# Five loads issued ahead of the sixth pair's q and k on SyncE's queue

## The chip, the cores and the metric

The kernel runs on one core of a Trainium2 chip. The metric is the device time of one execution in microseconds (us). The kernel before has a median of 680.91 us over 3 runs (680.24 to 683.12).

## The reference, cut to what matters

Two kinds of attention are added, and their sum goes through two mixers:

```
q, k, v: (4, 8, 576, 64)                 # batch, heads, positions, width of a head
q_d, k_d, v_d = means of 4 neighbouring rows of q, k, v       # 144 rows
out   = repeat(softmax(q_d k_d^T / 8) v_d, 4)                 # pooled attention
out  += softmax(q k^T / 8, only where |i - j| < 4) v          # local attention
x     = out as (4, 576, 512)
u     = x + (relu(x^T w_tok1) w_tok2)^T                       # token mixer
x     = u + relu(u w_ch1) w_ch2                               # channel mixer
theta = x w_theta;  y = w_tok_r (x cos theta) + w_tok_i (x sin theta)
result = (x + y) + relu((x + y) w_ch)
```

The weights arrive as 64-bit floats and are turned on the chip into pairs of a high and a low part, so that a product takes three matmuls.

## The kernel before, in words

The 32 heads are worked as 16 pairs of heads (4 for each batch) and as 8 quads (two pairs each). In the attention each step is a generator: every `next` issues the instructions up to its next `yield`. A string, ORDER (lines 33 to 84), holds the names of the steps in the order in which they are advanced, and so the order in which the instructions stand on each engine's queue; nothing rearranges them in this stage (it is recorded under `tc.manual_schedule`). The last stage (from line 1356 on) is arranged by a scheduler.

The steps that the change names, each with what its first advance issues on SyncE (SP):

- `P5` (`load_pair`, line 375): q and k of pair 5, 582 KB, into one of 4 buffers `qk` in rotation; the buffer is free when TensorE and VectorE have done with pair 1, whose q and k it held.
- `W0` (`load_values`, line 382): the values of pair 0 as four DMAs, two of 32 partitions (146.2 KB each) and two of 6 partitions (27.4 KB each).
- `G1`, `G0` (`tok1`, line 333): 512 KB each of w_tok1; `G6` (`tok2`, line 347): 288 KB of w_tok2. All go through `converted` (line 166), whose line 187 issues the DMA; the conversion is in later advances.
- `V1` (`pool_values`, line 391): the values of quad 1 to be pooled, 650 KB, into the single buffer `vd`; it is free when GpSimd (POOL) has done the second addition of quad 0 (line 401).

The later advances of these steps use the data: `K5` (`pool_pair`, lines 421 and 422) adds neighbouring columns of pair 5's q and k on VectorE (DVE); `V1`'s next advance adds on POOL (line 398); `G1`, `G0` and `G6` convert on ScalarE (ACT) at lines 199 and 201 and on DVE at lines 203 to 215. `F0` (`quad_front`, lines 425 to 520) is the pooled attention of quad 0: its products end in `od` on TensorE (PE, lines 493 to 500), DVE divides them (lines 504 to 507) into `ods`, SP stores `ods` to memory (lines 510, 511) and loads it back, repeated, as `xu` (lines 516, 519). `L0` to `L3` (`pair_local`) is the local attention, with its scores at line 533.

Each DMA of SP bumps one of eight semaphores in turn (DMAHW0 to DMAHW7 in the rows of the order below), and waits until the DMA that used this semaphore before it, eight DMAs earlier, has landed.

Of the kernel before, what the change touches and what calls it, by code (L numbers as in the profile page):

```python
# [30 lines left out]
FIRST = 1  # L31
ROWS = ((8, 9), (0, 2), (4, 6), (2, 3))
ORDER = """
G3 P0 G2 I*2 P1 G3 P4 G3 V0 P2 G3 K0 G3 G2 I G2 I L0*2 P3 K1 F0 W1 L0 F0 L1 L0 G3 F0 V0 L1*2 P5 V0 L2 W0 G2 K2 V0 G2
F0 G1 L1 V1 F0 L2 K3 G0 G6 K4 L0 F0 L0 L2 L1 G2 F1 L2 K5 L1 L0 F0 F1 G1*2 F1 V1 F0*2 W3 L0 F1 G5 G0 L1 G0 F1 G6 F2 L1
G0 P6 W2 G5 G6 L3 V1 F2 V1 L3 G6 F2 F1 L3 G1 G4 F1 L2 P7 L5 L2 L5 F1 G1 L3 A0 V2 X0 A1 T0 L3 G1 L5 G0 L3 T0 G0 L2 G2
F1 G4 F2 G5 T0 K6 T0 V2 X2 L2 G6 W5 F2 K7 V2 L4*2 E0.0*2 T0 L4 V3 V2 A2 L3 E0.1 L5 G4 L4 W4 L5 G6 L5 G4 L3 X2 F3 G5 P8
P9 A3 G4 F2 G5 E0.1 T1 G4 G5 T0 F2 V3 L4 F3 F2 T0 L4 V3 X2 F3 L6 V3 L6 X7 T0 P11 L6 X2 X0 F3 K8 U0.0 L6 T0 X2 X0 U0.0
# [1419 lines left out]
```

## Time and profile before

| what | value |
|---|---|
| median of 3 runs | 680.91 us (680.24 to 683.12) |
| the profiled execution's own time | 686.51 us |
| its span, from the first instruction to the last | 684.7 us |
| PE busy | 657.2 us (96%), 7320 matmuls |
| DVE, ACT, POOL busy | 521.0, 321.1, 98.0 us |
| DMA moved | 109.93 MB, mean 161 GB/s |

The profile is of one execution, which was 686.51 us long by itself; the trace covers 684.7 us of these, and 1.8 us lie outside. All positions below are microseconds from the start of the span. In the trace "SPq" is SP's queue: its rows are the issues of DMAs, and the data follow later. "issue" as the cause of an idle stretch means that nothing that the profile shows was waited for. PEclk is the granted clock of PE as a share of 2.4 GHz, so 0.50 is its lower level, 1.2 GHz.

### The profile page before, as it was taken

Reading aid. Unit: us, or ns where it says so; the run is one execution under the profiler, and the core shown is the slowest. Engines: PE = TensorE matmul, PEld = TensorE weight load, DVE = VectorE, ACT = ScalarE, POOL = GpSimd, SP = SyncE. Lnnn points to the kernel's source line nnn. Section 1 sums busy time; section 2 is a strip of 40 time slices with the busy share of each in tenths; the row PEclk is TensorE's granted clock in tenths of the full one; section 3 lists DMA queues with packets and bytes.
Section 4 is the critical chain, followed back from the end, with each engine's and each line's share of the span. In section 5 each row is a group of like instructions: output and inputs, shape, how many; then the busy total and the mean of one; then the engine's idle time right before and its main releaser. Section 6 shows DMA issues by size and latency. Waiting matters only on the chain.

```text
span 684.7 us, 17393 instructions
## 1 busy us (share of the span) xinstructions
PE 657.2 (96%) x7320; PEld 627.6 (92%) x7320; DVE 521.0 (76%) x952; ACT 321.1 (47%) x632; POOL 98.0 (14%) x92
## 2 busy tenths in 40 slices
PE   7678898999999999999999999999999999999997
PEld 4457788989999999999999999999999998998997
DVE  5789997878462679898987886668798848857837
ACT  4466657466252556434624423253657326526311
POOL 3034220604200242300200210012000000000000
PEclk9899999999999999999999999999999999999999
DMA  8688886777441866625353853599620240140202
GB/s 280 198 273 238 255 250 237 209 243 242 137 146 53 285 232 211 226 76 145 128 150 102 279 133 95 178 335 284 169 62 1 75 149 1 61 140 1 70 1 69
DMA packets 93021, 109.93 MB, mean 161 GB/s; under 512 B 46880, under 2 KB 69536, under 8 KB 92944
## 3 DMA queue, kind: packets, MB, share of 16 engines
q1 hardware_dynamic: 92080, 106.08, 49.8%
q0 software_dynamic: 864, 2.75, 1.0%
q8 instruction: 57, 0.93, 0.6%
q14 instruction: 20, 0.16, 0.1%
HBM read 79.13 MB, written 29.69 MB: 159 GB/s over the span
## 4 chain that ended last, share of the span: by engine, by line
PE 83%; DMA 6%; DVE 5%; ACT 3%; SPq 1%; issue 1%; DVEq 0%; ACTq 0%
PE y L158 6%; PE y L157 6%; PE y L159 6%; PE c L158 4%; PE c L157 4%; PE c L159 4%; PE c L699 4%; PE c L702 4%; PE c L700 4%; PE c_p L903 3%; PE c_p L905 3%; PE c_p L902 3%; PE th L158 2%; PE th L157 2%; PE th L159 2%; DMA qk<-qkT 2%
## 5 line engine op out<-in xcount | busy, mean ns | idle before, releaser
L158 PE MATMUL y<-wrl,zh 128*128 128x288 f32 x256 | 74.9, 296 | 0.0
L157 PE MATMUL y<-wrh,zh 128*128 128x288 f32 x256 | 74.8, 296 | 0.0
L159 PE MATMUL y<-wrh,zl 128*128 128x288 f32 x256 | 71.9, 295 | 0.0
L219 POOL TENSOR_TENSOR ww<-ww,raw 128x512 int32<-128x512 int32 (+2 forms) x30 | 41.1, 1373 | 161.8 <-DMA raw<-w_ch 55.6
L157 PEld LDWEIGHTS y<-wrh,zh 128*128 128x128 f32 x256 | 48.0, 188 | 0.0
L158 PEld LDWEIGHTS y<-wrl,zh 128*128 128x128 f32 x256 | 48.0, 188 | 0.0
L159 PEld LDWEIGHTS y<-wrh,zl 128*128 128x128 f32 x256 | 46.9, 188 | 0.0
L219 POOL TENSOR_TENSOR raw<-raw 128x512 int32<-128x512 int32 (+2 forms) x16 | 20.0, 1248 | 139.0 <-DVE raw L215 57.5
L1231 DVE TENSOR_TENSOR cx<-y,cx 128x288 f32<-128x288 f32 x32 | 14.6, 457 | 32.3 <-PE y L159 31.7
L151 ACT CAST cuh<-cx 128x288 fp32r<-128x288 f32 (+1 forms) x16 | 8.8, 553 | 59.5 <-DVE cx L1231 59.5
L199 ACT ACTIVATE ww<-raw 128x512 f32<-128x512 f32 (+2 forms) x30 | 19.4, 647 | 27.1 <-DVE c1l L223 9.5
L921 DVE SCALAR_TENSOR_TENSOR g<-c,g 128x384 fp32r<-128x384 f32 x40 | 21.1, 551 | 13.9 <-ACT g L918 13.8
L157 PE MATMUL th<-thh,cxh 128*128 128x512 f32 (+1 forms) x92 | 31.6, 343 | 0.0
L158 PE MATMUL th<-thl,cxh 128*128 128x512 f32 (+1 forms) x92 | 31.6, 343 | 0.0
L918 ACT ACTIVATE g<-c 128x384 fp32r<-128x384 f32 x40 | 19.1, 490 | 25.5 <-PE c L159 25.5
L159 PE MATMUL th<-thh,cxl 128*128 128x512 f32 (+1 forms) x92 | 31.1, 343 | 0.0
L201 ACT ACTIVATE raw<-raw 128x512 int32<-128x512 uint32 (+3 forms) x46 | 29.4, 639 | 0.0
L929 DVE TENSOR_TENSOR ut<-c,ut 128x384 f32<-128x384 f32 x32 | 17.1, 551 | 9.9 <-PE c L702 9.9
L533 PE MATMUL s<-qk 64*32 64x38 f32 x1280 | 16.1, 205 | 6.1 <-issue 6.1
L533 PEld LDWEIGHTS s<-qk 64*32 64x32 f32 x1280 | 13.6, 105 | 8.8 <-issue 8.4
L157 PE MATMUL t<-w2h,h 128*128 128x256 f32 (+1 forms) x64 | 21.5, 337 | 0.0
L157 PE MATMUL c<-uh,c1h 128*128 128x384 f32 x64 | 21.4, 334 | 0.0
(390 smaller groups left out, 2270.5 us busy)
## 6 DMA issues: line engine op xcount, KB each, us to landing
raw<-w_ch SPq DMA_DIRECT2D x27, 512.0 KB
qk<-qkT SPq DMA_DIRECT2D x16, 582.0 KB
xT<-ut SPq DMA_DIRECT2D x12, 768.0 KB
vd<-vtok SPq DMA_DIRECT2D x8, 650.0 KB
vw<-vloc SPq DMA_DIRECT2D x32, 146.2 KB
uT<-us SPq DMA_DIRECT2D x16, 288.0 KB
ut<-uT SPq DMA_DIRECT2D x6, 768.0 KB
ut<-xT SPq DMA_DIRECT2D x6, 768.0 KB
```

Of the source, the lines that this page charges most:

```text
L157: pe.matmul(out, lh, rh, start=start, stop=False, skip_group_check=again)
L158: pe.matmul(out, lh, rl, start=False, stop=False, skip_group_check=again)
L159: pe.matmul(out, ll, rh, start=False, stop=stop, skip_group_check=again)
L201: act.activation(f, words[:, :, 0], AF.Copy, scale=2.0**-29)
L219: pool.tensor_tensor(out=w.bitcast(I32), in0=w.bitcast(I32), in1=f, op=ALU.add)
L533: pe.matmul(s[r : r + 32, j, i // 2 * W : i // 2 * W + W], q[64 * j : 64 * j + 64, 32 * g : 32 * g + 32], k[64 * j : 64 * j + 64, 32 * g : ...
L699: pe.matmul(ps[:, 0:MIX], h[:, cb % 2, d], h1, start=cb == cbs[0], stop=False)
L700: pe.matmul(ps[:, 0:MIX], l[:, cb % 2, d], h1, start=False, stop=False)
L702: pe.matmul(ps[:, 0:MIX], weight[cb // 2][2][:, cb % 2, d], h2, start=False, stop=cb == cbs[-1])
L902: pe.matmul(ps[:, 0:MIX], h[:, cb % 2, d], h1, start=cb == cbs[0], stop=False)
L903: pe.matmul(ps[:, 0:MIX], l[:, cb % 2, d], h1, start=False, stop=False)
L921: dve.scalar_tensor_tensor(out=h2, in0=ps, scalar=0.0, in1=h1.bitcast(F32), op0=ALU.max, op1=ALU.subtract)
```

## The change

Five steps, `W0`, `G1`, `G0`, `G6` and `V1`, are advanced for the first time ahead of `P5`; in the kernel before, `P5` stands first and the others are spread over what follows. No instruction is added or taken away. The core of the diff (one line of the string before, and the same place now):

```
-... G3 F0 V0 L1*2 P5 V0 L2 W0 G2 K2 V0 G2
-F0 G1 L1 V1 F0 L2 K3 G0 G6 K4 L0 F0 L0 ...
+... G3 F0 V0 L1*2 V0 L2 W0 G1 G0 G6 V1 P5
+G2 K2 V0 G2 F0 L1 F0 L2 K3 K4 L0 F0 L0 ...
```

On SP, between the values of pair 1 (`vw_1`) and the store of quad 0's pooled output (`od`), before. Here `qk_1` is P5's load (pair 1 of the second batch), `vw_0` are W0's, `raw` are G1's, G0's and G6's, `vd_1` is V1's:

```order
L378 DMA qk_1_347<-qkT 128x1164 [waits DMAHW6_49,DVE_49,PE_49]
L387 DMA vw_0_366<-vloc 32x1170 [waits DMAHW7_49]
L387 DMA vw_0_366<-vloc 32x1170 [waits DMAHW0_49]
L387 DMA vw_0_366<-vloc 6x1170 [waits DMAHW1_49]
L387 DMA vw_0_366<-vloc 6x1170 [waits DMAHW2_49]
L187 DMA raw_393<-w_tok 128x2x256 [waits DMAHW3_49]
L396 DMA vd_1_396<-vtok 128x1300 [waits DMAHW4_49,Pool_49]
L187 DMA raw_444<-w_tok 128x2x256 [waits DMAHW5_49]
L187 DMA raw_446<-w_tok 128x288 [waits DMAHW6_49]
L510 DMA od_0_57<-ods_0_572 4x32x256 [waits DMAHW7_49,DVE_49]
```

The same place on SP now:

```order
L387 DMA vw_0_364<-vloc 32x1170 [waits DMAHW6_49]
L387 DMA vw_0_364<-vloc 32x1170 [waits DMAHW7_49]
L387 DMA vw_0_364<-vloc 6x1170 [waits DMAHW0_49]
L387 DMA vw_0_364<-vloc 6x1170 [waits DMAHW1_49]
L187 DMA raw_369<-w_tok 128x2x256 [waits DMAHW2_49]
L187 DMA raw_371<-w_tok 128x2x256 [waits DMAHW3_49]
L187 DMA raw_373<-w_tok 128x288 [waits DMAHW4_49]
L396 DMA vd_1_375<-vtok 128x1300 [waits DMAHW5_49,Pool_49]
L378 DMA qk_1_377<-qkT 128x1164 [waits DMAHW6_49,DVE_49,PE_49]
L510 DMA od_0_57<-ods_0_572 4x32x256 [waits DMAHW7_49,DVE_49]
```

The wait for PE and DVE moved from the head of the nine loads to their end, and each of the other eight waits for a semaphore that was used one DMA earlier. From the store of `od` on SP's queue is the same in both.

On DVE, around the first use of P5's data, now; the rows before are the same but for the numbers in the names:

```order
L545 TENSOR_REDUCE mx_2_490<-s_2_349 128x10 [waits PE_49]
L546 TENSOR_TENSOR pbuf_119<-s_2_349,mx_2_490 128x2x5x38 [waits DVE_49,PE_49,Activation_49]
L223 TENSOR_TENSOR w1l<-raw_141,w1h 128x256 [waits Activation_49]
L421 TENSOR_TENSOR qa_1_522<-qk_1_377 128x576 [waits DMAHW6_49]
L422 TENSOR_TENSOR qkd_0_448<-qa_1_522 128x288 [waits DVE_49]
L504 TENSOR_SCALAR rd_0_569<-od_0_458 128x5 [waits PE_49]
L505 RECIPROCAL rd_0_569<-rd_0_569 128x5 [waits DVE_49]
L507 TENSOR_TENSOR ods_0_572<-od_0_458,rd_0_569 128x320 [waits DVE_49]
L452 TENSOR_REDUCE mxd_1_574<-sd_1_500 128x4 [waits PE_49]
```

Nothing moved here: `K5`'s two additions stand ahead of the division that makes `ods`. PE, ACT and POOL keep their order in the attention too. In the last stage the scheduler places some rows of `y`, `o` and `th` differently on PE (rows 2703 to 3102 of 4013), and on DVE and ACT the additions and casts around them.

## Rows read from the trace of the kernel before

**Rows 1.** Windows: busy us (x instructions) of each engine, PEclk, DMA share, GB/s.
```profile
107.00:680.62 573.62, 572.91 (x4870) 559.07 (x4868) 432.56 (x786) 260.47 (x490) 66.50 (x57) 1.00 0.46 144
21.11:27.94 6.83, 5.28 (x78) 3.89 (x86) 4.04 (x8) 1.23 (x4) 1.60 (x1) 0.50 0.71 262
106.45:109.86 3.41, 3.41 (x11) 3.41 (x12) 3.26 (x9) 2.20 (x8) 0.00 (x0) 0.50 0.63 169
```

**Rows 2.** Chain that ended last, 0 to 150 us: start, us, what.
```profile
19.04 3.63 issue
...
35.58 4.70 DMA raw<-w_tok
```

**Rows 3.** Timeline of ACT: start, us, line, tiles, xcount [idle before <-releaser].
```profile
28.52 0.69 ACT L199 ACTIVATE raw<-raw 128x512 f32<-128x512 f32 x1
...
40.30 0.46 ACT L199 ACTIVATE ww<-raw 128x288 f32<-128x288 f32 x1 [4.72 <-DMA raw<-w_tok]
```

**Rows 4.** Timeline of SP's queue, 9 to 36 us.
```profile
9.87 1.61 SPq L387 DMA_DIRECT2D vw<-vloc  x4
15.31 0.36 SPq L378 DMA_DIRECT2D qk<-qkT  x1
...
16.64 0.32 SPq L387 DMA_DIRECT2D vw<-vloc  x1
...
17.34 0.40 SPq L187 DMA_DIRECT2D raw<-w_tok  x1
17.84 0.41 SPq L396 DMA_DIRECT2D vd<-vtok  x1
...
20.22 0.33 SPq L187 DMA_DIRECT2D raw<-w_tok  x1
...
28.27 0.62 SPq L510 DMA_DIRECT2D od<-ods  x1
```

**Rows 5.** SP's waits, 9 to 28 us: total us, times, longest us.
```profile
SPq L187 <- DMA qk<-qkT: 1.5, 1, 1.5
```

**Rows 6.** Timeline of DVE, 24 to 30 us.
```profile
25.15 0.75 DVE L421 TENSOR_TENSOR qa<-qk 128x576 f32<-128x576 f32 x1
25.94 1.48 DVE L422 TENSOR_TENSOR qkd<-qa 128x288 f32<-128x288 f32 x1
...
27.75 0.49 DVE L507 TENSOR_TENSOR ods<-od,rd 128x320 f32<-128x320 f32 x1
29.02 0.76 DVE L452 TENSOR_REDUCE mxd<-sd 128x4 f32<-128x576 f32 x1 [0.77 <-PE sd L443]
```

**Rows 7.** Timeline of DVE and POOL: the same addition undisturbed, and POOL's beside it.
```profile
19.73 0.46 DVE L422 TENSOR_TENSOR qkd<-qa 128x288 f32<-128x288 f32 x1
...
11.92 1.34 POOL L398 TENSOR_TENSOR vd<-vd 128x650 f32<-128x650 f32 x1 [5.62 <-DMA vd<-vtok]
...
25.49 1.60 POOL L398 TENSOR_TENSOR vd<-vd 128x650 f32<-128x650 f32 x1 [10.04 <-DMA vd<-vtok]
```

**Rows 8.** Timeline of PE, 22 to 44 us.
```profile
26.14 0.44 PE L500 MATMUL od<-vs,pts 128*32 128x65 f32 x8
...
32.46 0.76 PE L477 MATMUL pdt<-fixed,pd 128*128 128x128 f32 x5 [2.65 <-ACT pd L473]
...
39.91 0.30 PE L500 MATMUL od<-vs,pts 128*32 128x65 f32 x8
43.12 0.77 PE L558 MATMUL pt<-fixed,pbuf 128*128 128x128 f32 x5 [2.91 <-ACT pd L473]
```

**Rows 9.** Windows again, for the rate of the DMA engines (last number, GB/s).
```profile
13.50:16.00 2.50, 1.56 (x72) 1.18 (x55) 0.72 (x3) 1.45 (x5) 1.95 (x3) 1.00 0.60 155
...
19.00:21.50 2.50, 0.04 (x2) 0.00 (x0) 1.15 (x2) 0.26 (x1) 0.00 (x0) 0.92 1.00 201
21.50:23.50 2.00, 0.84 (x7) 0.76 (x8) 0.45 (x1) 0.00 (x0) 0.00 (x0) 0.50 1.03 399
...
25.50:27.50 2.00, 2.00 (x45) 1.76 (x37) 1.96 (x3) 0.00 (x0) 1.60 (x1) 0.50 0.19 65
```

More of the change, by code (lines that the diff above doesn't have):

```diff
@@ L33 @@
 ORDER = """
-G3 P0 G2 I*2 P1 G3 P4 G3 V0 P2 G3 K0 G3 G2 I G2 I L0*2 P3 K1 F0 W1 L0 F0 L1 L0 G3 F0 V0 L1*2 P5 V0 L2 W0 G2 K2 V0 G2
-F0 G1 L1 V1 F0 L2 K3 G0 G6 K4 L0 F0 L0 L2 L1 G2 F1 L2 K5 L1 L0 F0 F1 G1*2 F1 V1 F0*2 W3 L0 F1 G5 G0 L1 G0 F1 G6 F2 L1
+G3 P0 G2 I*2 P1 G3 P4 G3 V0 P2 G3 K0 G3 G2 I G2 I L0*2 P3 K1 F0 W1 L0 F0 L1 L0 G3 F0 V0 L1*2 V0 L2 W0 G1 G0 G6 V1 P5
+G2 K2 V0 G2 F0 L1 F0 L2 K3 K4 L0 F0 L0 L2 L1 G2 F1 L2 K5 L1 L0 F0 F1 G1*2 F1 V1 F0*2 W3 L0 F1 G5 G0 L1 G0 F1 G6 F2 L1
 G0 P6 W2 G5 G6 L3 V1 F2 V1 L3 G6 F2 F1 L3 G1 G4 F1 L2 P7 L5 L2 L5 F1 G1 L3 A0 V2 X0 A1 T0 L3 G1 L5 G0 L3 T0 G0 L2 G2
```

## The prediction

> **What bounds the kernel now.** I read the windows first. From 107 us until PE's last matmul at 680.62 us PE is busy for 572.91 of 573.62 us [rows 1]: behind 107 us there are 0.7 us to be had, and whatever comes earlier or later at the start shifts the whole rest. All nine moved loads stand before 21 us, so I then followed the chain of waits through the first 50 us. It shows two large pieces: 3.63 us from 19.04 us in which PE stands for "issue", and from 35.58 to 40.28 us a load of a weight [rows 2]. The second is the one that counts: ACT stands 4.72 us for it at 40.30 us [rows 3], and behind it PE waits 2.91 us for ACT at 43.12 us [rows 8]. That load is issued at 35.58 us [rows 2] because SP's queue, which is in order, goes on only when the pooled output `ods` is there: SP stores it at 28.27 us, right after the division that DVE starts at 27.75 us and ends at 28.24 us [rows 4, 6]; from there to 35.58 us SP only issues and waits for this store. So the end follows the time at which DVE ends `ods`, one for one.
>
> What sets `ods`? DVE's order. Before the division stand the two additions on P5's data, lines 421 and 422, at 25.15 and 25.94 us, and the second takes 1.48 us [rows 6]; the products it divides start their last group on PE at 26.14 us for 0.44 us [rows 8], so they are there before DVE is.
>
> **The change part by part.** No work is added or removed: 0 us on each engine. What moves is nine DMA issues on SP.
>
> *The five loads that move up.* Before, P5 waits for PE until 15.31 us, with SP free since 11.48 us (9.87 + 1.61) [rows 4]. Now W0 takes its place. But each DMA waits for the landing of the one eight places before. Before, W0's third piece waited for pair 3's q and k and went at 16.64 us [rows 4]; now this wait falls on its fourth piece. So three pieces of W0 go some 4 us earlier, between about 11.5 and 13.5 us, the fourth at about 16.6, and behind it, at 0.4 us each, G1 at 16.9 (before 17.34), G0 at 17.3, G6 at 17.8 (20.22) and V1 at 18.1 (17.84, so no earlier). What is this worth? G1's first reader, ACT at 28.52 us, has no idle time before it [rows 3]; PE reads W0 behind `od`. Only POOL waited, for V1, until 25.49 us [rows 7], and V1 doesn't come earlier. So 0 us.
>
> *P5 moves down.* It goes at about 18.5 us instead of 15.31 (PE and DVE, for which it waits, are done at 15.31, so it holds nobody on SP; behind it stands the store of `od`, 10 us away), and behind 1962 KB of G1, G0, G6 and V1. When does it land, T? With its own 582 KB that makes 2544 KB, or 2.61 MB, from the issue at 16.9 us. Before, the nine loads, 2891 KB or 2.96 MB, took from 15.31 us to about 25.9 us (from 25.5 to 27.5 us only 65 GB/s still flow [rows 9]): 10.6 us with the start, 279 GB/s. At this pace T = 16.9 + 2.61/0.279 = 16.9 + 9.4 = 26.3 us.
>
> The bounds of T: the fastest is data without a gap and at 399 GB/s, the rate of 21.5 to 23.5 us [rows 9]: 16.9 + 6.5 = 23.4 us. For the slowest I take the start from P5 itself: G6 waited for it 1.5 us, until 20.22 us [rows 4, 5], so it took 4.91 us, of which 0.60 MB at 399 GB/s are 1.5; 3.4 us are start. Then a stretch as from 19.0 to 21.5 us at 201 GB/s (0.50 MB), which like that from 13.5 to 16.0 us at 155 GB/s comes where the 32-partition and 6-partition pieces of a pair's values are on the way [rows 9], and the rest at 399 GB/s, 5.3 us: 16.9 + 3.4 + 2.5 + 5.3 = 28.1 us. I take 26.3, since the same loads made this pace in the same queue.
>
> *DVE with P5 at T.* Line 421 had its data before 25.15 us; now it waits for them, and behind it in DVE's order line 422, the division, and the maximum of quad 1. From T: 0.79 us to line 422, then 0.46 us and not 1.48. The 1.48 us stand where POOL's addition on V1 runs from 25.49 us for 1.60 us; undisturbed the one takes 0.46 and the other 1.34 us [rows 6, 7]. V1 lands now ahead of P5 by P5's own 1.5 us, so POOL's 1.34 us are over when line 422 comes. Then 0.82 us from the end of line 422 (27.42) to the end of `ods` (28.24). New end: 26.3 + 0.79 + 0.46 + 0.82 = 28.37 us, against 28.24: +0.1 us. With T at its bounds: 25.5 us, -2.8 (the products must then be ready at 24.6 us, which needs PE's stall of 3.63 us to vanish), and 30.1 us, +1.9.
>
> The Trainium skill, page "SBUF — State Buffer", section "Who interferes with whom", says more than this row: a DVE instruction with two SBUF inputs and a GpSimd instruction that reads SBUF exclude each other for the whole instruction, whichever starts first. By that rule line 421 itself, started while POOL's addition runs, would wait for its end, which no run here shows (its row at 25.15 us started before POOL's); it would cost up to 1.3 us, and that is a rival below.
>
> *PE's stall.* What it waits for from 19.04 us on the profile doesn't name. It may shrink with other traffic around it, wholly (-3.6 us) or not at all. I cost it at nothing either way: PE's next wait is for ACT at 32.46 us, 2.65 us long [rows 8], and ACT follows DVE's maximum of quad 1 at 29.02 us [rows 6], which stands behind `ods`. What PE gains at 22 us it stands at 32 us. That maximum waited 0.77 us for PE [rows 6], and can come up to that much earlier; SP's chain does not see it.
>
> *The last stage.* The scheduler reorders some products there. PE has 0.7 us idle in 573.62 [rows 1], so a gain is at most that; I take 0.
>
> Sum: +0.1 us. On the profiled execution (span 684.7, 686.51 us by itself, 5.6 above the median of the runs) 686.6; on the median, 680.91 + 0.1 = 681.0 us.
>
> **The rivals.**
>
> A, faster: the nine loads stream without a gap and PE's stall goes. For it: SP stood 3.8 us before 15.31 us while the rate fell to 155 GB/s [rows 4, 9]. Against it: the wait on the eighth DMA before holds SP until 16.6 us still. `ods` ends 2.8 us earlier, and PE, whose idle time then lies elsewhere, may keep 2.4 GHz from 106.45 to 109.86 us, where it was granted 0.50 and busy throughout [rows 1], worth 3.41/2 = 1.7 us. 680.91 - 4.5 = 676.4 us.
>
> B, slower: PE starves. If its stall shrinks and P5 is late, PE is through with its work early and stands for up to 2.65 + 3.63 = 6.3 us before 32.46 us. In this trace it idled 3.63 us from 19.04 us and had 0.50 of its clock from 21.11 to 27.94 us [rows 1, 2]. Such a 6.83 us at 1.2 GHz over the work from 32.46 us loses 3.4 us; the wait at 43.12 us covers 2.91 of it for `pt`, but quad 1's products, whose last group starts at 39.91 us [rows 8], would be late by the whole, and quad 1's `ods` with its store on SP behind them. With T half-way to its slow end, +1.0: 680.91 + 3.4 + 1.0 = 685.3 us. It decides from the point where P5 lands after about 27 us and PE's idle time before 32.46 us exceeds the 3.63 us. Against it: 2.65 and 2.91 us of idle time were not followed at once by a lower clock.
>
> C, the shared port: V1 and P5 land together, line 421 waits for POOL: 681.0 + 1.3 = 682.3 us.
>
> **How the numbers follow.** Forecast 0.62, A 0.13, B 0.20, C 0.05. Half a per cent of 680.91 is 3.4 us, about what a measurement of this kernel can tell from no change: below 677.5 faster, above 684.3 slower. A is faster, B slower, forecast and C are the same: 0.13, 0.67, 0.20. The forecast's own bounds are 680.91 - 2.8 = 678.1 and 680.91 + 1.9 = 682.8 us; the range goes from 678.1 to 684.2, to the edge of B, and leaves A and most of B out.
>
> **What would show it.** In the profile after: W0's first issues at about 11.5 us and its last at about 16.6; P5's issue near 18.5; a wait of DVE's line 421 for the DMA of `qk`, ended near 26.3; line 422 at 0.46 us; SP's store of `od` within 1 us of 28.3 and ACT's wait for `raw<-w_tok` ended near 40.4. The prediction is wrong if `od` is stored before 27 or after 29.5 us, if PE's clock falls in a new stretch after 30 us with work in it, or if the start of PE's unbroken stretch near 107 us moves by other than `od`'s shift.

## The result and the profile after

The kernel after takes 686.77 us (median of 13 runs, 683.55 to 690.76), the kernel before, beside it, 682.19 us (13 runs, 679.75 to 684.18): a ratio of 1.0064, with a 95% interval of 1.0042 to 1.0086. It is slower by 4.4 us (2.9 to 5.9), where I had forecast no change (681.0 us on the 680.91 of the kernel before, with a range of 678.1 to 684.2).

The profiled execution of the kernel after happens to be the fastest of its 13 runs (683.55 us), and that of the kernel before was a long one (686.51 us). So what one trace shows may be the luck of one execution: in that of the kernel after `od` is stored 1.4 us later than in [rows 4], and yet PE ends 3.0 us earlier. Below I read the first trace of the kernel after for the mechanism, and for sizes the means over five traces of it and three of kernels in which P5 goes first.

DVE after, timeline from 27 us (start, us, line, tiles, idle before and what ended it), which answers to [rows 6]:

```profile
27.57 0.76 DVE L421 TENSOR_TENSOR qa<-qk 128x576 f32<-128x576 f32 x1 [5.71 <-DMA qk<-qkT]
28.37 0.46 DVE L422 TENSOR_TENSOR qkd<-qa 128x288 f32<-128x288 f32 x1
...
29.16 0.49 DVE L507 TENSOR_TENSOR ods<-od,rd 128x320 f32<-128x320 f32 x1
29.57 0.75 DVE L452 TENSOR_REDUCE mxd<-sd 128x4 f32<-128x576 f32 x1
```

DVE stands 5.71 us for P5, with the division and the maximum of quad 1 behind it. Here T is 27.57 us. SP's queue after [rows 4]:

```profile
14.53 0.27 SPq L387 DMA_DIRECT2D vw<-vloc  x1
...
17.12 0.27 SPq L387 DMA_DIRECT2D vw<-vloc  x1
17.44 1.96 SPq L187 DMA_DIRECT2D raw<-w_tok  x3
19.49 0.38 SPq L396 DMA_DIRECT2D vd<-vtok  x1
19.98 0.36 SPq L378 DMA_DIRECT2D qk<-qkT  x1
29.68 0.61 SPq L510 DMA_DIRECT2D od<-ods  x1
...
33.26 0.60 SPq L516 DMA_DIRECT2D xu<-od  x1
...
37.00 0.35 SPq L187 DMA_DIRECT2D raw<-w_tok  x1
```

W0's third piece is held until 14.53 us, its last until 17.12 us; G1 follows at 17.44, and P5 goes at 19.98 us, 1.5 us behind the forecast. What the DMA engines moved meanwhile, by windows (the last number is GB/s), beside [rows 9]:

```profile
16.00:17.40 1.40, 1.40 (x14) 1.17 (x12) 1.37 (x3) 0.53 (x1) 0.00 (x0) 1.00 0.20 60
17.40:20.00 2.60, 1.71 (x99) 1.22 (x97) 2.46 (x5) 0.97 (x2) 0.00 (x0) 1.00 0.61 199
20.00:22.00 2.00, 2.00 (x65) 1.59 (x65) 1.63 (x4) 1.08 (x3) 0.00 (x0) 1.00 0.80 209
22.00:24.00 2.00, 2.00 (x72) 1.64 (x61) 0.00 (x0) 1.22 (x4) 0.00 (x0) 1.00 1.04 410
```

While SP waits ahead of 17.12 us, the engines run dry: 60 GB/s. In the trace of the packets G1's first one begins only at 18.49 us. PE after [rows 2, 8]:

```profile
19.93 0.26 PE L533 MATMUL s<-qk 64*32 64x38 f32 x4 [0.89 <-issue]
...
26.40 1.07 PE L568 MATMUL o<-vw,plt 38*32 38x65 f32 x65 [2.28 <-issue]
33.01 1.33 PE L477 MATMUL pdt<-fixed,pd 128*128 128x128 f32 x5 [5.54 <-ACT pd L473]
...
43.19 0.77 PE L558 MATMUL pt<-fixed,pbuf 128*128 128x128 f32 x5 [1.05 <-ACT pd L473]
```

The stall of 3.63 us has shrunk to 0.89, a second one of 2.28 us stands at 26.40 us where the kernel before has none, and PE stands 5.54 us ahead of quad 1's transposes instead of 2.65. ACT's wait for the weight [rows 3] ends where it did before in this trace, though the weight was issued 1.42 us later (37.00 us against 35.58), since its load took 3.3 us and not 4.70:

```profile
40.33 0.48 ACT L199 ACTIVATE ww<-raw 128x288 f32<-128x288 f32 x1 [3.23 <-DMA raw<-w_tok]
```

By windows [rows 1], PE is still full from 107 us on, and two stretches were granted 0.50 of the clock:

```profile
107.00:677.65 570.65, 570.13 (x4863) 556.46 (x4861) 431.74 (x781) 259.92 (x489) 66.12 (x57) 1.00 0.46 144
26.77:37.01 10.24, 4.71 (x170) 3.69 (x162) 7.61 (x19) 4.87 (x13) 2.30 (x3) 0.50 0.29 92
54.08:57.49 3.41, 3.41 (x92) 3.33 (x92) 3.31 (x8) 0.00 (x0) 0.00 (x0) 0.50 1.00 252
```

In the first, PE works for 4.71 of 10.24 us only. I count work at half the clock as taking twice its time, so that PE loses half of its busy time in such stretches (the five transposes at 33.01 us take 1.33 us in one, and 0.76 us outside of one in [rows 8], so this is a little high, for either kernel): (4.71 + 3.41)/2 = 4.1 us here, and (5.28 + 3.42 + 3.41)/2 = 6.1 us in the kernel before ([rows 1]; its third stretch, 48.42 to 51.84 us, is busy throughout).

### The profile page after: what moved, and what is told of

It reads as the page before. It is cut to its first block, busy times and chain, and to the rows that moved or that the text cites. A ratio compares the mean times of both kernels' runs of the same rounds, so it can differ in the third digit from the quotient of the medians.

```text
span 681.8 us, 17394 instructions
## 1 busy us (share of the span) xinstructions
PE 655.7 (96%) x7320; PEld 625.9 (92%) x7320; DVE 518.4 (76%) x952; ACT 320.4 (47%) x632; POOL 97.4 (14%) x92
## 4 chain that ended last, share of the span: by engine, by line
PE 84%; DVE 6%; DMA 5%; ACT 2%; SPq 1%; issue 1%; DVEq 0%; ACTq 0%
PE y L158 6%; PE y L157 6%; PE y L159 6%; PE c L158 4%; PE c L157 4%; PE c L159 4%; PE c L699 4%; PE c L700 4%; PE c L702 4%; PE c_p L902 3%; PE c_p L905 3%; PE c_p L903 3%; DMA qk<-qkT 3%; PE th L158 2%; PE th L159 2%; PE th L157 2%
## 5 line engine op out<-in xcount | busy, mean ns | idle before, releaser
L159 PE MATMUL c<-uh,c1l 128*128 128x384 f32 x64 | 21.4, 334 | 0.0
L158 PE MATMUL c<-ul,c1h 128*128 128x384 f32 x64 | 21.4, 334 | 0.0
```

Source lines behind the costliest of these rows:

```text
L158: pe.matmul(out, lh, rl, start=False, stop=False, skip_group_check=again)
L159: pe.matmul(out, ll, rh, start=False, stop=stop, skip_group_check=again)
```

## The experiments

Two theories stood at the start. "Wait", later called "output", is my own step: P5 lands late, `ods` with it, and the end follows through the store of `ods`. "Clock" is my rival B: PE stands so long that what follows is done at 1.2 GHz. A third, "grouping", was that the five loads side by side cost something by themselves. Ratios are to the kernel before on the same chip, with 95% intervals.

**The two kernels again.** c1 is the kernel before and c2 the kernel after, unchanged.

> The kernel before once more, so that its granted clocks stand beside those of the kernel after. Theory 'clock' (P5's late landing leaves PE without work, and the work behind it is done at 1.2 GHz in most executions): the time is 682 us, and the mean granted clock of most runs is near 0.989, against a middle of 0.983 in the runs of the kernel after; 4.6 us of difference are worth 2 x 4.6 x 0.5 / 684 = 0.0067 of mean clock. Theory 'wait' (DVE's wait for P5 alone shifts the end, one for one): the clocks are the same as in the kernel after, within 0.002, and the difference lies in when the unbroken stretch of PE starts.

> The kernel after once more, for a second trace of it. Theory 'clock': 686.8 us; if the profiled execution is a usual one, its mean clock is near 0.983, and about 4 us more than in the first trace of it are lost in stretches at 1.2 GHz with work in them before 110 us. Theory 'wait': the trace has the same stretches at 1.2 GHz as the first one, and the pooled output of quad 0 is stored later than at 29.68 us.

Measured: c1 683.84 us, 0.9989 (0.9969 to 1.0009); c2 688.54 us, 1.0064 (1.0035 to 1.0093). The middle of the mean clocks was 0.9875 in c1 and 0.9855 in c2 (0.983 in the 13 runs of the result): lower in the kernel after, but by less than the 0.0067 that "clock" needs. In c1 the store of `ods` and what follows on SP stand earlier than in [rows 4]:

```profile
27.34 0.61 SPq L510 DMA_DIRECT2D od<-ods  x1
...
30.91 0.60 SPq L516 DMA_DIRECT2D xu<-od  x1
```

So 28.27 us, on which my sum rested, was itself a late execution. In c2 T is 27.93 us.

**Which move costs.** e1 puts P5 back ahead of the loads, e2 moves P5 alone.

```
e1, against the kernel after:
-... L1*2 V0 L2 W0 G1 G0 G6 V1 P5
+... L1*2 P5 V0 L2 W0 G1 G0 G6 V1
e2, against the kernel before:
-... L1*2 P5 V0 L2 W0 ... K3 G0 G6 K4
+... L1*2 V0 L2 W0 ... K3 G0 G6 P5 K4
```

> The changed kernel with P5 put back ahead of the five loads, so that against the kernel before only V1 stands behind G1, G0 and G6 instead of behind G1. Theories 'clock' and 'wait': both hang on P5, which lands as before, so 682.2 us, within 1 us, and clocks near 0.989. Rival 'grouping' (the five loads side by side with V1 late are what costs): as the kernel after, 686 to 687 us.

> The kernel before with P5 alone moved behind G6, the five loads in their old order W0, G1, V1, G0, G6. Theories 'clock' and 'wait': P5 lands as late as in the kernel after, so 686 to 687 us; 'clock' with a mean clock near 0.983, 'wait' near 0.989. Rival 'grouping': 682 us. Rival 'last stage' (the scheduler's other order of the last products costs the 4.6 us): this kernel has a last order of its own, so any time, but the start of the unbroken stretch of PE as in the kernel before.

Measured: e1 683.70 us, 1.0001 (0.9980 to 1.0021); e2 689.62 us, 1.0074 (1.0050 to 1.0098). Grouping costs nothing that these runs can tell; P5's place costs it all. The middle of e2's mean clocks was 0.983, as "clock" had expected; what such a mean is worth is taken up below. DVE in e2 waits for P5 even longer:

```profile
28.83 0.76 DVE L421 TENSOR_TENSOR qa<-qk 128x576 f32<-128x576 f32 x1 [6.42 <-DMA qk<-qkT]
```

**Taking the wait off.** e3 moves the additions `K5` behind the division and quad 1's maximum in the kernel after; e4 does so in the kernel before.

```
-... L2 K5 L1 L0 F0 F1 G1*2 ...
+... L2 L1 L0 F0 F1 K5 G1*2 ...
```

> The changed kernel with DVE's additions on P5's data put behind the division of quad 0 and the maximum of quad 1, so that only they wait for P5. Theory 'wait': the products are there at 22.3 us in both traces of the kernel after, so the pooled output is stored near 23.5 us instead of 29.7, and the time falls by at least the 2 us that it is later in the kernel after than in the kernel before: a ratio below 1.001. Theory 'clock' alone: PE's idle time before the transposes falls from 5.5 to about 2 us and with it the loss, so a ratio near 1.002 or below with a mean clock near 0.9875. A rival 'data' (what is late is not DVE's place in line but P5's data for PE itself, for quad 2 and pair 5): the ratio stays at 1.006.

> The kernel before with the same move of the additions. In its traces DVE comes to them at 24.1 to 25.2 us with the data there, and they take 2.3 us, or 1.2 where POOL is not beside them; the last product of the division starts at 26.14 us for 0.44 us. Theory 'wait' (one for one): the store is 0.5 to 1.2 us earlier, the time 0 to 1.2 us shorter, a ratio of 0.998 to 1.000. Theory 'clock' alone: 1.000.

Measured: e3 684.05 us, 0.9992 (0.9968 to 1.0015); e4 685.34 us, 0.9989 (0.9961 to 1.0016). e4's interval holds what either theory expected of it. In e3 the loss is gone, so P5's data are not needed early by anyone else. But a store 4.2 us earlier than the 27.3 us of P5-first traces brought no gain that is clear of noise. One reason is that the store then goes among loads still under way. SP's queue in e3:

```profile
23.12 0.61 SPq L510 DMA_DIRECT2D od<-ods  x1
...
29.27 0.59 SPq L516 DMA_DIRECT2D xu<-od  x1
```

The way to `xu` takes 6.15 us here and 3.57 us in c1: `xu` is only 1.6 us earlier than in c1, and of these too the time shows nothing clear.

**Which of the two paths behind P5.** e7 lets only the maximum wait for P5, e8 only the division.

```
-... L2 K5 L1 L0 F0 F1 G1*2 ...
+... L2 L1 L0 F0 K5 F1 G1*2 ...      (e7)
+... L2 F1 K5 L1 L0 F0 G1*2 ...      (e8)
```

> The changed kernel with the additions on P5's data behind the division of quad 0 but still ahead of the maximum of quad 1: the pooled output no longer waits for P5, quad 1's maximum does. Theory 'output' (the step of the prediction: the end follows the end of `ods`, through its store and the weight load behind it): the store goes at 23.1 us as in the kernel with both ahead, and the ratio is about 0.999. Rival 'maximum' (the loss goes through quad 1's maximum, ACT's exponentials and PE's transposes, which start near 32.5 to 33.5 us): the ratio is 1.004 to 1.006 although the store is 6 us early.

> The other half: quad 1's maximum ahead of the additions on P5's data, the division behind them. Theory 'output': the store stays at 29.5 to 30 us and so does the ratio, at 1.006, though PE's transposes start near 27.5 us. Rival 'maximum': the ratio falls to 0.999 to 1.002. If each of the two paths carries the loss by itself, this kernel and the one with the additions in between both stay above 1.003.

Measured: e7 685.02 us, 1.0012 (0.9975 to 1.0048); e8 688.87 us, 1.0056 (1.0029 to 1.0083). e7 stores `od` at 23.16 us and issues `xu` at 28.62. PE starts the transposes as late as in the kernel after, yet most of the loss seems gone (the interval doesn't quite shut out 1.004). SP's queue and PE in e7:

```profile
23.16 0.61 SPq L510 DMA_DIRECT2D od<-ods  x1
...
33.62 1.33 PE L477 MATMUL pdt<-fixed,pd 128*128 128x128 f32 x5 [4.92 <-ACT pd L473]
```

In e8 they start at 28.35 us, and nothing is won that is clear of noise: `od` is stored at 30.96 us, and ACT then stands for the weight behind that store. SP's queue and ACT in e8:

```profile
30.96 0.61 SPq L510 DMA_DIRECT2D od<-ods  x1
...
42.33 0.46 ACT L199 ACTIVATE ww<-raw 128x288 f32<-128x288 f32 x1 [9.88 <-DMA raw<-w_tok]
```

This is the plainest row of the study: with the maximum out of the way, the whole wait (9.88 us) stands where "output" puts it. So the path through the store is enough by itself for the loss; that the path through the maximum carries none of it is not shown.

**The clock.** e5 and e11 fill PE's idle time ahead of quad 1's transposes with matmuls on zeros.

```
+        if Q == 1:
+            warm(mmp.tile([128, 512], F32, tag="mm", name="fill")[:, 0:320], 36)     (14 in e11)
         pt = wide(f"pdt_{at}")
```

> The changed kernel with 36 idle matmuls (128x320 into a PSUM tile that nobody reads, about 0.145 us each, 5.2 us) set ahead of quad 1's transposes, in the 5.5 to 6.9 us in which PE stands there; nothing else moves. Theory 'clock' (half of the loss or more is work done at 1.2 GHz behind this idle time): the stretch of 10.24 us at 1.2 GHz that begins between 26 and 29 us goes or shrinks to 3.4 us, the mean clock rises by 0.003 to 0.004 to that of the kernel before, and the time falls by 1.2 to 2.4 us against the kernel after, to about 686.5 us here, a ratio of 1.003 to 1.005 to the kernel before. Theory 'wait' (the later pooled output of quad 0 is the whole loss): no gain, the ratio stays at 1.0064.

> The changed kernel with 14 idle matmuls ahead of quad 1's transposes: 2.0 us at 2.4 GHz, 4.1 us at 1.2 GHz, so inside PE's 5.5 us of idle time at either. Theory 'clock' (the rest of the loss is work at 1.2 GHz that follows this idle time): mean clock near 0.9875, ratio 1.003 to 1.004. Theory 'output': the clock may change, the ratio stays at 1.006 to 1.007.

Measured: e5 694.77 us, 1.0126 (1.0092 to 1.0160); e11 689.14 us, 1.0053 (1.0029 to 1.0077). e5 was badly made: the fill itself fell to 1.2 GHz, ran past the time at which PE was wanted, and was followed by a new stall. PE in e5:

```profile
28.09 7.64 PE L315 MATMUL fill<-zero 128*128 128x320 bf16 x36
35.57 0.71 PE L479 MATMUL pdt<-fixed,pd 128*128 128x128 f32 x5
...
47.71 0.32 PE L500 MATMUL od<-vl,pts 128*32 128x65 f32 x1 [4.57 <-issue]
```

It tells nothing of the theories. e11 leaves PE's start alone (33.36 us, after 3.21 us of idle time), but its interval holds both expectations, so it doesn't decide either. The middle of its mean clocks was 0.9845 and not the 0.9875 that "clock" named.

**Three more traces of the kernel after**, because c2 and the first trace had fallen on executions with a high mean clock.

> The kernel after, one trace. Theory 'clock': in an execution with a mean clock of 0.980 to 0.985, 17 to 27 us before 110 us are at 1.2 GHz, and PE's matmuls in them lose 6 to 9 us, against 4.1 us in both earlier traces of this kernel and 4.8 to 7.9 us in the three of kernels with P5 first. Theory 'output': those stretches lie on idle time, the matmuls lose 4 to 6 us, and the pooled output goes at 29.5 to 31 us.

> As the look before: 'clock' 6 to 9 us lost where the mean clock is 0.980 to 0.985, 'output' 4 to 6 us.

> As the look before: 'clock' 6 to 9 us lost where the mean clock is 0.980 to 0.985, 'output' 4 to 6 us.

Measured: 690.84, 688.16 and 688.19 us, mean clocks 0.982, 0.988 and 0.982; T 28.44, 28.16 and 28.45 us; `od` stored at 30.54, 30.26 and 30.56 us. Stretches at half the clock in c3, by windows (PE's busy time is the first number behind the length):

```profile
26.34:39.99 13.65, 7.32 (x210) 5.44 (x210) 9.62 (x24) 4.96 (x13) 3.97 (x4) 0.50 0.35 107
50.23:53.65 3.42, 3.42 (x33) 2.66 (x27) 3.32 (x7) 3.33 (x10) 0.88 (x1) 0.50 0.67 232
77.54:84.37 6.83, 6.71 (x120) 6.46 (x121) 4.86 (x11) 3.96 (x11) 3.36 (x3) 0.50 0.69 198
```

and in c1, the kernel before:

```profile
22.20:25.62 3.42, 3.42 (x62) 2.44 (x62) 2.76 (x5) 1.18 (x3) 0.78 (x1) 0.50 1.00 385
32.44:35.86 3.42, 3.42 (x110) 2.43 (x91) 3.00 (x6) 1.51 (x4) 2.48 (x3) 0.50 0.83 271
42.68:52.92 10.24, 8.94 (x182) 7.45 (x181) 8.29 (x13) 7.69 (x18) 3.25 (x3) 0.50 0.93 315
```

PE loses (7.32 + 3.42 + 6.71)/2 = 8.7 us in c3 at a mean clock of 0.982, and (3.42 + 3.42 + 8.94)/2 = 7.9 us in c1 at 0.987. By the letter c3 and c5 (8.2 us) meet what "clock" expected of them. But c1 shows what that expectation lacked: the kernel before loses nearly as much at a higher mean clock, since in c3 some 6 us of the first slow stretch have no work in them. A lower mean clock over idle time costs nothing.

Over the traces, with PE's idle time up to its last matmul (us, means; P5 first: the kernel before, c1, e1; P5 last: the kernel after, c2 to c5):

| | T, DVE's start on P5 | store of `od` | issue of `xu` | transposes | idle | lost at 1.2 GHz | PE's end |
|---|---|---|---|---|---|---|---|
| P5 first | no wait | 27.3 | 30.9 | 31.0 | 21.2 | 6.3 | 678.35 |
| P5 last | 28.1 | 30.2 | 33.8 | 33.5 | 24.6 | 6.0 | 681.54 |

`od` is 2.9 us later, `xu` 2.9, PE's idle time grows by 3.4, its end by 3.2, and the loss at 1.2 GHz by nothing in the mean. The interval of the result (2.9 to 5.9 us) holds that. But the loss at 1.2 GHz ranges from 4.1 to 8.7 us in single traces, so a share of a microsecond or two for "clock" is not shut out.

The delay can be followed to PE along the path that "output" names. ACT's wait for the weight, in c1 and in c2:

```profile
38.64 0.49 ACT L199 ACTIVATE ww<-raw 128x288 f32<-128x288 f32 x1 [4.70 <-DMA raw<-w_tok]
...
41.98 0.49 ACT L199 ACTIVATE ww<-raw 128x288 f32<-128x288 f32 x1 [4.51 <-DMA raw<-w_tok]
```

Over the eight traces this wait ends at 39.0 us in the mean with P5 first and at 41.8 with P5 last, and the products `pt` behind it [rows 8] start at 41.8 and 44.7 us: 2.9 us again. In the first trace of the kernel after neither moved (40.33 and 43.19 us), which is why one trace would have misled here.

**A better place for P5.** e6 puts it directly behind W0, e9 behind W0 and G1; e10 is e6 once more.

```
-... L2 W0 G1 G0 G6 V1 P5
+... L2 W0 P5 G1 G0 G6 V1      (e6, e10)
+... L2 W0 G1 P5 G0 G6 V1      (e9)
```

> The changed kernel with P5 directly behind W0 and ahead of G1, G0, G6 and V1: issued near 16.9 us instead of 19.98. By the bytes ahead of it it lands some 3 us earlier than in the kernel after, at 24.5 to 25 us, about when DVE comes to the additions in the kernel before. Theory 'wait': the pooled output is stored at 26.5 to 27.5 us and the ratio is 1.000, within 0.002. A rival by which any place behind W0 costs the same (P5 is slow whatever stands ahead of it, since the values' small pieces are on the way): the ratio is 1.005 or above.

> The changed kernel with P5 behind W0 and G1, so between the kernel with P5 directly behind W0 (its data came at 22.9 us) and the kernel after (27.6 to 27.9 us). P5 is issued near 18.9 us. If T is set by the bytes ahead of it, DVE's wait for P5 ends between 24 and 25.5 us, the store of the pooled output goes at 26.1 to 27.6 us, and the ratio is 0.997 to 1.001. If T jumps as soon as another load is ahead of P5, the wait ends at 27 us or later and the ratio is 1.004 or above.

> The kernel with P5 directly behind W0 once more (its first interval was 0.9915 to 0.9988). If its gain is real: a ratio of 0.993 to 0.998, DVE's wait for P5 ended near 23 us, PE's wait for its instructions at 19 us at 0.6 us instead of 3 us, and PE idle for less than 4 us between 23 and 34 us. If it was chance: 1.000, within 0.001.

Measured: e6 682.60 us, 0.9951 (0.9915 to 0.9988); e10 684.46 us, 0.9968 (0.9937 to 0.9998); e9 683.62 us, 0.9994 (0.9959 to 1.0028). Both intervals of the order with P5 second lie below 1, so it beats both kernels, the one before by 2.2 to 3.4 us (the medians of the two runs). P5's data came at 22.88 and 22.30 us, earlier than the 24.5 that I had expected of e6, and e6's ratio lies below the 0.998 that "wait" allowed. DVE's wait in e6:

```profile
22.88 0.77 DVE L421 TENSOR_TENSOR qa<-qk 128x576 f32<-128x576 f32 x1 [1.00 <-DMA qk<-qkT]
```

and PE in e6:

```profile
19.89 0.26 PE L533 MATMUL s<-qk 64*32 64x38 f32 x4 [0.64 <-issue]
...
28.31 1.33 PE L477 MATMUL pdt<-fixed,pd 128*128 128x128 f32 x5 [0.81 <-ACT pd L473]
```

P5 lands 4.7 us earlier than in the kernel after, PE keeps the short stall, and it hardly stands at the transposes (0.81 us). A second stall for "issue", 2.55 us at 26.63 us (none, 0.24 and 1.74 us there with P5 first), takes a part back. Why this order beats the kernel before is read from these rows; no run tests it by itself. In e9 DVE's wait ends at 23.41 us, before the 24 to 25.5 that I had expected, and in e10 at 22.30: 512 KB ahead of P5 cost 0.5 to 1.1 us, and the 1450 KB of G0, G6 and V1 another 4 to 5.

## Why the prediction was wrong, step by step

- **The step that failed: "P5 moves down", the landing at 26.3 us.** It came at 27.6, 27.9, 28.2, 28.4 and 28.5 us, 28.1 in the mean, which is the slow bound that I had worked out and not taken. That it is met to the tenth is chance: the bound counts from G1 at 16.9 us, and G1 went at 17.35 to 17.67. In the first trace 0.5 us come from G1's issue (17.44 instead of 16.9), since W0's last piece had to wait until 17.12 us, and 0.7 from the pace: 2.61 MB in 10.1 us are 258 GB/s, not 279. In the mean of the five it is 0.6 us from G1's issue (17.5) and 1.2 from the pace (10.6 us, 246 GB/s). I had taken the pace of the old order, in which P5's q and k filled the engines from 15.31 us; in the new one SP stands, the engines run dry, and they start again with G1: 60 GB/s from 16.0 to 17.4 us and 199 from 17.4 to 20.0, where hardly any of the values is left on the way (36 KB). So the values' small pieces, to which I had put down the slow stretch of my bound, are not its cause here. Why the rate is only 209 GB/s from 20 to 22 us, with nothing but weights on the way, stays open.
- **The base, 28.24 us, came from one execution.** The store was at 28.27, 27.34 and 26.30 us in three traces with P5 first. Forecast +0.1, plus 1.8 for T, plus 1.0 for the base, makes the 2.9 us that were measured at the store. The medians differ by 4.4 us (2.9 to 5.9); what of the rest is real stays open.
- "DVE with P5 at T" was right to the hundredth: 2.07 us from T to the end of `ods` forecast, 29.65 - 27.57 = 2.08 measured; line 422 at 0.46 us. Rival C played no part: line 421 starts 0.02 to 0.03 us after the signal that P5 has landed in every trace with P5 last, in e2 too, where POOL's addition had ended at 26.54 us, 2.3 us earlier. In the kernel after POOL's addition ends at 27.52 us and P5 lands at 27.55, since V1's and P5's data come one behind the other.
- "The end follows `ods` one for one" held for a delay, in the mean of the traces: 2.9 us at the store, 3.2 at PE's end; e8 shows that this path is enough. It didn't hold for a gain: e3 and e7 store 4 us earlier than the kernels with P5 first and end with them. The slower way from `od` to `xu` (6.15 and 5.46 us instead of 3.57) takes 1.9 to 2.6 us of that; the rest (`xu` is 1.6 and 2.3 us earlier than in the mean of P5 first) their times don't show, though with intervals of 3 to 5 us they hardly shut it out.
- "What PE gains at 22 us it stands at 32 us" was right in these two traces: 2.7 us shorter there, 2.9 longer here. That I costed the moved-up loads at 0 fits e1 and e2: grouped behind P5 they cost nothing, and with the loads in their old order P5's late place costs as much as in the kernel after.
- The last stage: +0.0. From 107 us on PE idles 0.52 us after, 0.71 before, in the first trace of each.
- Rival B named the size (685.3 us) and the condition (P5 after about 27 us), but only 1.0 of the 4.4 us of its sum was T's delay. The other 3.4 us, work at 1.2 GHz, the traces don't show; so it is luck that its 4.4 us are those of the medians. Of my signs, `od` stored after 29.5 us was the one that spoke. A slow stretch with work in it after 30 us came too (54.08 to 57.49 us), but kernels with P5 first have such stretches as well (42.68 to 52.92 in c1), so it says nothing. The end of ACT's wait near 40.4 us looked as forecast in the first trace, and came at 41.7 to 42.9 us in c2 to c5.

## What to carry to other kernels

Before a load is put behind others in a queue, ask which instruction waits for it and what stands behind that instruction on its in-order engine: here two additions whose result nobody needed yet held a division, a store and a weight load. Take the landing time of the load at its slow end where its order of issue changes what fills the engines, and take the base for such a sum from more than one execution. When two orders are compared by the granted clock, count PE's work in the slow stretches, not their length.

## What the runs showed of the hardware

- PE's "issue" stall at 19 us goes with the place of P5: 2.8 to 3.6 us in four traces with P5 issued near 15 us, 0.25 to 1.4 in all others. In the trace of the packets a 16 KB packet of the queue for instructions (q8) begins 2.3 to 2.9 us before PE goes on: at 19.75 us in the kernel before (PE at 22.66), at 17.57 after (19.93). That holds in all traces but e11, where the packet begins at 16.37 us and PE's stall ends at 19.58. That this packet is what PE waits for, and that it is late behind P5's data, is a reading of these times; it wasn't tested by itself.
- The way of `od` from SP's store to the issue of `xu` takes 3.57 us in both kernels, 4.20 in e6, 5.46 in e7 and 6.15 in e3, where loads of weights and V1, in e3 and e7 P5 too, are still under way.
- Single executions with P5 first differ by 2 us in when `ods` is stored (26.30 to 28.27 us), nearly as much as this change moves it.
- Line 422 took 1.48 us in the kernel before and 1.57 us in c1, each time beside POOL's addition on V1, and 0.46 us in all other traces that I compared. POOL's addition ended at 27.09 and 26.18 us there, and line 422 at 27.42 and 26.49, so 0.33 and 0.31 us behind it: DVE's addition got little done until POOL's was over. That agrees with the Trainium skill, page "SBUF — State Buffer", section "Who interferes with whom", by which a DVE instruction with two SBUF inputs and a GpSimd instruction that reads SBUF exclude each other, and the one that starts second waits for the whole of the other.
